# Six big loads get a wait on a later VectorE instruction: attention and a token-mixing MLP on one Trainium2 core

## The chip, the cores and the metric

The kernel runs on one core of one Trainium2 chip. The core has five engines with a queue of instructions each: TensorE (PE in the profile, with its weight loads as PEld), VectorE (DVE), ScalarE (ACT), GpSimd (POOL) and SyncE (SP). SP and POOL are used here mainly to issue DMA transfers, and all transfers run on the core's 16 DMA engines. The metric is the device time of one execution in microseconds. The kernel before was run three times: 746.62, 742.23 and 740.57 us, median 742.23.

## The reference

One input x of 2048 rows and 640 columns is normalised by row. It goes through a self-attention with 32 heads of 20 columns and, beside it, through an MLP that mixes rows (tokens) rather than columns. The result is x plus the attention's output times silu of the MLP's output.

```python
def _A_ref(x, wqkv, wo):                     # 32 heads, Dh = 20
    qkv = (x @ wqkv).reshape(B, S, 3, H, Dh)  # S = 2048
    q, k, v = ...
    p = softmax(einsum("bhqd,bhkd->bhqk", q, k) * Dh ** -0.5)
    o = einsum("bhqk,bhkd->bhqd", p, v)
    return o.reshape(B, S, D) @ wo
def _B_ref(x, w1, b1, w2, b2):
    h = layernorm(x)
    u = gelu(einsum("bsd,sf->bdf", h, w1) + b1)   # w1: 2048 x 1536
    return (einsum("bdf,fs->bds", u, w2) + b2).transpose(0, 2, 1)   # w2: 1536 x 2048
xn = layernorm(A_x)
return A_x + _A_ref(xn, ...) * silu(_B_ref(xn, ...))
```

## The kernel before

**The planner.** The program is not written in the order in which it runs. `_Kern.schedule` builds jobs (scores, exponentials, products with v, the MLP, the output projection) and picks the next instruction of each engine with a clock of its own. Each instruction or transfer is a `_Task` with an engine, a start `t0` and an end `fin` on that clock, and the tasks that it has to wait for (`waits`, one per counter). `klg` holds, for each counter, how far a task is known to be done once this one is done. At the end `emit` writes each engine's tasks in order: first one semaphore wait for each entry of `waits`, then the instruction. Only tasks with `need_inc` raise their semaphore. What runs on the chip is a fixed order for each engine and a fixed set of waits; the planner's clock only chose them.

**The attention.** The heads are taken in 8 groups of four, and the queries in four blocks of 512. For each key chunk of 128 the scores of a head go to a PSUM bank (line 1362). Three quarters of the exponentials are ACT's (line 1392, into pt_sb). The others are made on DVE as bit patterns: line 1403 turns scores into a 16-bit pattern in dt_sb, and then three shifted copies of that tile are needed. A copy is made either on DVE (line 1471, adding a constant) or by an accumulating DMA that adds a constant tile from HBM to the tile in place (`emit_x`, line 1434, task names dX...). That accumulating transfer is issued by POOL; it moves 512 KB. It works in place, so it starts only when PE has read the tile's earlier state, and PE waits for its landing before it reads the tile again. The products with v (line 1497) read pt_sb and dt_sb, and accumulate four copies of a tile with scaled v (v_sb, vs_sb).

**The MLP.** It runs as bank jobs between the attention's instructions: m1_0 to m1_11 with w1, a gelu on ACT, then m2_0 to m2_15 with w2 (lines 715 and 723; results picked up at lines 887 and 896, then lines 920 to 925). The weights come in pieces of two column chunks: w1_0 to w1_5 (1024 KB each, line 850) and w2_0 to w2_7 (768 KB each, line 857), in two slots of regA. Piece k is loaded when the chunks that used piece k - 2 are done, so w1_2 goes out behind m1_1 and is read by m1_4 and m1_5.

**SP's queue.** SP issues all other transfers in the planner's order, and a task that waits holds up all behind it. Of interest are the weight pieces, the load of wo (line 1794) and the four small pieces of line 1797 right behind it, the last x rows for the residual (x2_3, line 1789, into regA), the four stores of each pass's attention output (line 1639), the stores and loads of q and k through HBM (lines 745, 770 and 784), and late in the program 16 transposing loads (line 1006). Transfers use eight counters in turn, so a transfer also waits for the one eight places ahead.

Of the kernel before, what the change touches and what calls it, by code (L numbers as in the profile page):

```python
# [283 lines left out]
class _Kern:  # L284
# [8 lines left out]
    AB = 6  # L293
    JB = 7
    EVJ = 36.0
    XRES = 12
    RC = (1, 4, 7, 10, 13)
    NT = 2
# [66 lines left out]
        ("JOBF", (4, 0, 8)),  # L365
        ("EVJ", (36.0, 19.0, 45.0)),
        ("XLEFT", (16, 20, 14, 28, 99)),
# [33 lines left out]
    def __init__(self, nc, A_x, A_wqkv, A_wo, B_w1, B_b1, B_w2, B_b2, out):  # L401
# [10 lines left out]
        self.FC = self.F // 128  # L412
        self.prog = Prog(nc)

    def build(self):
        nc = self.nc
        pr = self.prog
        S, NB, FC = self.S, self.NB, self.FC
        es = ExitStack()
        with es:  # L420
            E = es.enter_context
            bf, f32, u16 = dt.bfloat16, dt.float32, dt.uint16
            t = {}

            def sb(name, shape, d):
                t[name] = E(nc.sbuf_tensor(name, shape, d))

            sb("wqk_sb", [P, 5, 2, 640], bf)
            sb("wp_sb", [P, 5, 2, 128], bf)
            sb("qs_sb", [P, self.NQS, 512], bf)  # L430
            sb("wv_sb", [P, 5, 640], bf)
            sb("xnT_sb", [P, 5, S], bf)
            sb("regA", [P, NB, self.D], bf)
            sb("regB", [P, FC, self.D], bf)
            sb("regC", [P, NB, self.D], bf)
            sb("qk_sb", [P, 2, 2, S], bf)
            sb("v_sb", [P, NB, self.H, 22], bf)
            sb("vs_sb", [P, 2, 3, len(self.RC), 88], bf)
            sb("pt_sb", [P, self.RP, 512], bf)
            sb("dt_sb", [P, self.NTILE, 4, 512], u16)  # L440
            sb("kc_sb", [P, 2, 64], u16)
            sb("zt_sb", [P, 2, 2, self.D], bf)
            sb("tr_sb", [P, 512], f32)
            sb("on_sb", [P, 16, 32], bf)
            sb("rden_sb", [P, 16], f32)
            sb("stage_sb", [P, 3, 512], bf)
            sb("idb_sb", [P, P], bf)
            sb("zw_sb", [P, 32], bf)
            sb("bst_sb", [P, NB, 12], f32)
            sb("st_sb", [P, 8, NB], f32)  # L450
            sb("cst_sb", [P, 4], f32)
            sb("b1h_sb", [P, FC], f32)
            sb("b2h_sb", [P, NB], f32)
            sb("bload_sb", [P, FC + NB], bf)
            t["ps_all"] = E(nc.psum_tensor("ps_all", [P, 4096], f32))
            t["qk_dram"] = nc.dram_tensor("qk_scratch_dram", [2, 560, S], bf)
            t["oT_dram"] = nc.dram_tensor("oT_scratch_dram", [8 * P, S], bf)
            t["kc_dram"] = nc.dram_tensor("kc_scratch_dram", [2 * P, 2048], dt.uint8)
            t["ok_dram"] = nc.dram_tensor("ok_scratch_dram", [S, 512], bf)
            sems = {}  # L460
            for e in ("pe", "act", "dve", "pool", "sp"):
                sems[e] = E(nc.semaphore(f"sem_{e}"))
            for i in range(pr.n_lanes):
                sems[f"d{i}"] = E(nc.semaphore(f"sem_d{i}"))
            for i in range(pr.NXL):
                sems[f"x{i}"] = E(nc.semaphore(f"sem_x{i}"))
            self.t = t
            self.schedule()
            pr.final_waits()
            pr.emit(sems)  # L470
# [6 lines left out]
    def schedule(self):  # L477
        pr, t, nc = self.prog, self.t, self.nc
# [594 lines left out]
        def res_steps(b):  # L1073
            def make(bk):
                r = regC[:, b, :]
                xa = regA[:, b, :]
                if b < self.XRES:
                    return [("xdma", lambda e: e.dma_start(r, A_x[0, b * 128:(b + 1) * 128, :], accum_op=ALU.add),
# [649 lines left out]
        for b in range(NB):  # L1728
            at = self.V1A + (self.V1B - self.V1A) * b / NB
            rest.append((at, f"v1_{b}", v_steps(b, 1), xtag(b // 4), 40.0, at))  # L1730
        for i, (a0, a1) in enumerate(self.QC):
            o = [(1, tb) for tb in range(4)] + [(0, tb) for tb in range(4)]
            for n, (w, tb) in enumerate(o if i < 4 else o[:4]):
                at = a0 + (a1 - a0) * n / (8.0 if i < 4 else 4.0)
# [4 lines left out]
        for G in range(1, NG):  # L1739
            cs = sorted({(80 * G - 80) // 128, (80 * G - 1) // 128})  # L1740
            for w in (1, 0):
# [5 lines left out]
                    at=(4 * G - 1.0 if G < NG - 1 else 24.0))  # L1747
# [35 lines left out]
        for gb in range(4):  # L1783
            if 4 * gb + 4 <= self.XRES:
                x2.append(("tag", f"x2_{gb}"))
# [407 lines left out]
        def do_step(j, eng):  # L2193
            s = j.steps[j.i]
            j.i += 1
            if s[0] == "ev":
                n = s[8]
                fn = ev_fn(s, eng)
                cost = ac(n) if eng == "act" else (dv(n, 0.53) if s[7].startswith("xTe") else dp(n))
                getattr(pr, eng)(fn, reads=s[5], writes=s[6], name=s[7], cost=cost)  # L2200
                if eng == "dve":
                    done_cost["dve"] += cost
            elif s[0] == "pe":
                done_cost["pe"] += s[5]
                if len(s) > 6:
                    c = pe_cost("pv", s[5])
                    for fn in s[1]:
                        pr.pe(fn, reads=s[2], writes=s[3], name=s[4], cost=c / len(s[1]), w=s[5] / len(s[1]))
                else:
                    pr.pe(s[1], reads=s[2], writes=s[3], name=s[4], cost=pe_cost("full", s[5]), w=s[5])  # L2210
            else:
                getattr(pr, s[0])(s[1], reads=s[2], writes=s[3], name=s[4], cost=s[5])
                if s[0] in done_cost:
                    done_cost[s[0]] += s[5]
            settle(j)

        def eng_cands(eng, T):
            c = []
            for j in active:
                s = j.steps[j.i]  # L2220
                if s[0] == eng:
                    p_ = min(j.prio, self.EVJ) if eng == "dve" and j.bk is not None and not ramp[0] else j.prio
                    c.append((p_, pr.ready(eng, s[2], s[3]), lambda j=j: do_step(j, eng)))
# [41 lines left out]
        while True:  # L2265
# [41 lines left out]
            r, e = bt  # L2307
# [5 lines left out]
        assert nclaim[0] == NALL and not avail and not dquads and not jobs and not bankq and not active, (  # L2313
            nclaim[0], len(avail), len(dquads), [j.name for j in jobs][:9], [j.name for j in bankq][:9],
            [j.name for j in active][:9], pv_pass, pv_left)
        self.model = dict(pr.T)
        self.stats = stats

# [35 lines left out]
```

## Time and profile before

| | us |
|---|---|
| three runs, median | 742.23 |
| lowest and highest run | 740.57, 746.62 |
| the profiled execution's own time | 746.19 |
| its span in the profile | 744.4 |
| mean granted TensorE clock, as a share of full | 0.995 |

The rows shown below are of one profiled execution. A row of a timeline gives start and length in us, the engine, the line of the kernel, the operation, the tile written and the tile read, how many instructions are merged in the row, and in brackets how long the engine was idle before it and what ended that. SPq and the POOL rows of line 1434 are issues of transfers; how long a transfer takes from issue to landing is told in a row of its own. A row of a table by stretch gives the stretch, its length, and the busy time of PE, PEld, DVE, ACT and POOL with the number of instructions, then the granted TensorE clock, the busy share of the DMA engines and the GB/s. A busy PE is not PE at its peak, since matmuls are pipelined.

### The profile page before, as it was taken

Reading aid. Unit: us, or ns where it says so; the run is one execution under the profiler, and the core shown is the slowest. Engines: PE = TensorE matmul, PEld = TensorE weight load, DVE = VectorE, ACT = ScalarE, POOL = GpSimd, SP = SyncE. Lnnn points to the kernel's source line nnn. Section 1 sums busy time; section 2 is a strip of 40 time slices with the busy share of each in tenths; the row PEclk is TensorE's granted clock in tenths of the full one; section 3 lists DMA queues with packets and bytes.
Section 4 is the critical chain, followed back from the end, with each engine's and each line's share of the span. In section 5 each row is a group of like instructions: output and inputs, shape, how many; then the busy total and the mean of one; then the engine's idle time right before and its main releaser. Section 6 shows DMA issues by size and latency. Waiting matters only on the chain.

```text
span 744.4 us, 23686 instructions
## 1 busy us (share of the span) xinstructions
PE 709.4 (95%) x10506; PEld 236.9 (32%) x10520; DVE 701.0 (94%) x1286; ACT 715.5 (96%) x711; POOL 91.5 (12%) x107
## 2 busy tenths in 40 slices
PE   8889999999989999999899999899999999999997
PEld 7332222222322232322322323233333333332233
DVE  7989999999978999989889999899999999999997
ACT  5999999999989999999999999999999999999995
POOL 4300000100002001001101001110110101102311
PEclk9999999999999999999999999999999999999999
DMA  8767544542456554455463446824668785445443
GB/s 238 147 129 106 122 77 92 85 83 48 86 118 113 84 118 80 92 118 105 77 140 50 90 65 131 181 44 121 130 128 132 129 157 116 82 105 98 92 90 92
DMA packets 134091, 79.90 MB, mean 107 GB/s; under 512 B 84564, under 2 KB 123860, under 8 KB 133940
## 3 DMA queue, kind: packets, MB, share of 16 engines
q0 software_dynamic: 11808, 38.67, 28.6%
q1 hardware_dynamic: 122180, 39.71, 25.3%
q8 instruction: 82, 1.34, 0.8%
q14 instruction: 21, 0.17, 0.1%
HBM read 44.72 MB, written 10.75 MB: 75 GB/s over the span
## 4 chain that ended last, share of the span: by engine, by line
ACT 69%; PE 17%; DMA 6%; DVE 6%; issue 1%; SPq 0%; DVEq 0%
ACT pt_sb L1392 67%; PE ps_all L1497 5%; PE ps_all L1362 5%; DMA dt_sb<-kc_scratch_dram 4%; PE ps_all L715 4%; DVE dt_sb L1403 2%; PE ps_all L1036 1%; ACT zt_sb L920 1%; ACT regB L907 1%; DMA regA<-in_A_x_dram 1%; DVE dt_sb L1471 1%; DMA xnT_sb<-oT_scratch_dram 1%; DMA xnT_sb<-regC 1%; DMA oT_scratch_dram<-stage_sb 1%; DVE bst_sb L596 0%
## 5 line engine op out<-in xcount | busy, mean ns | idle before, releaser
L1392 ACT ACTIVATE pt_sb<-ps_all 128x1024 bf16<-128x1024 f32 (+1 forms) x682 | 692.1, 1210 | 12.0 <-PE ps_all L1362 9.4
L1403 DVE TENSOR_SCALAR dt_sb<-ps_all 128x512 uint16<-128x512 f32 x540 | 357.3, 680 | 24.6 <-PE ps_all L1362 16.3
L1362 PE MATMUL ps_all<-qk_sb 32*128 32x512 bf16 (+1 forms) x2128 | 269.5, 377 | 15.1 <-ACT pt_sb L1392 13.7
L1471 DVE TENSOR_SCALAR dt_sb<-dt_sb 128x2048 uint16<-128x2048 uint16 x335 | 222.3, 685 | 3.9 <-PE ps_all L1497 2.8
L1362 PEld LDWEIGHTS ps_all<-qk_sb 32*128 32x128 bf16 x2128 | 68.0, 91 | 274.2 <-ACT pt_sb L1392 222.7
L1497 PE MATMUL ps_all<-dt_sb,vs_sb 128*21 128x512 bf16 (+1 forms) x1668 | 144.0, 379 | 4.8 <-DMA dt_sb<-kc_scratch_dram 4.5
L1434 POOL DMA_DIRECT2D dt_sb<-kc_scratch_dram x70 | 64.9, 928 | 576.6 <-PE ps_all L1497 248.4
L1497 PE MATMUL ps_all<-pt_sb,v_sb 128*21 128x512 bf16 (+1 forms) x1572 | 120.6, 375 | 1.4 <-DVE v_sb L1190 0.8
L715 PE MATMUL ps_all<-regC,regA 128*32 128x128 bf16 (+1 forms) x1432 | 69.9, 296 | 1.5 <-issue 1.5
L715 PE MATMUL ps_all<-regB,regA 128*32 128x512 bf16 (+1 forms) x1464 | 65.7, 297 | 1.1 <-DVE qs_sb L765 0.6
L1497 PEld LDWEIGHTS ps_all<-dt_sb,vs_sb 128*21 128x21 bf16 x1668 | 36.1, 90 | 63.3 <-issue 39.7
L1497 PE MATMUL ps_all<-dt_sb,v_sb 128*21 128x512 bf16 (+1 forms) x556 | 53.3, 378 | 0.1
L715 PE MATMUL ps_all<-xnT_sb,wqk_sb 128*32 128x512 bf16 x640 | 48.9, 383 | 0.2 <-DVE v_sb L1190 0.2
L1497 PEld LDWEIGHTS ps_all<-pt_sb,v_sb 128*21 128x21 bf16 x1572 | 28.4, 91 | 42.7 <-issue 33.2
L723 PE MATMUL ps_all<-regC,regA 32*128 32x512 bf16 x104 | 40.4, 388 | 0.0
L715 PEld LDWEIGHTS ps_all<-regC,regA 128*32 128x32 bf16 x1432 | 27.6, 96 | 23.8 <-issue 14.6
L715 PEld LDWEIGHTS ps_all<-regB,regA 128*32 128x32 bf16 x1464 | 27.1, 96 | 25.1 <-issue 12.9
L723 PE MATMUL ps_all<-regB,regA 32*128 32x512 bf16 x72 | 27.7, 384 | 0.0
L1036 PE MATMUL ps_all<-wv_sb,xnT_sb 128*128 128x128 bf16 (+1 forms) x148 | 25.0, 294 | 2.4 <-issue 0.9
L1625 DVE STREAM_TRANSPOSE tr_sb<-ps_all 128x512 f32<-128x512 f32 x31 | 21.9, 707 | 0.1
L715 PE MATMUL ps_all<-wv_sb,xnT_sb 128*32 128x480 bf16 x320 | 21.8, 369 | 0.0
L1497 PEld LDWEIGHTS ps_all<-dt_sb,v_sb 128*21 128x21 bf16 x556 | 13.7, 90 | 20.2 <-issue 16.0
(88 smaller groups left out, 339.9 us busy)
## 6 DMA issues: line engine op xcount, KB each, us to landing
dt_sb<-kc_scratch_dram POOLq DMA_DIRECT2D x70, 512.0 KB, 6.3
regA<-in_B_w_dram SPq DMA_DIRECT2D x6, 1024.0 KB
regA<-in_B_w_dram SPq DMA_DIRECT2D x8, 768.0 KB
qk_sb<-qk_scratch_dram SPq DMA_DIRECT2D x56, 80.0 KB
qk_scratch_dram<-qs_sb SPq DMA_DIRECT2D x32, 128.0 KB
regA<-in_A_x_dram SPq DMA_DIRECT2D x3, 640.0 KB
ok_scratch_dram<-on_sb SPq DMA_DIRECT2D x96, 20.0 KB
regC<-in_A_x_dram POOLq DMA_DIRECT2D x12, 160.0 KB, 4.4
```

Source lines behind the costliest of these rows:

```text
L715: fns.append(lambda e, c=c, e_=e_: e.matmul(oc(c, e_), lhsT[:, c:e_], rhs, start=start, stop=stop, tile_position=(0, c)))
L723: row = lambda g: (lambda e: e.matmul(oc(0, 128), lhsT[32 * g:32 * g + 32, :], rhs[32 * g:32 * g + 32, :], start=False, stop=False, tile_p ...
L907: steps.append(("act", lambda e, d=d: e.activation(d, d, AF.Gelu_apprx_tanh), [S_(f"u{f}_{q}") for f in range(f0, f0 + 3) for q in (0, 1)] ...
L920: steps.append(("act", lambda e: e.activation(tt_, z, AF.Tanh), sz, [stt], f"th2_{j}", ac(n)))
L1036: steps.append(("pe", lambda e, c=c: e.matmul(ap, oT_sb[:, c, b * 128:(b + 1) * 128], wo_ap[:, c, c0:c0 + n], start=(opens and c == 0), st ...
L1362: t = pr.pe(lambda e, outp=outp, lhsT=lhsT, rhs=rhs, g=g: e.matmul(outp, lhsT, rhs, start=True, stop=True, tile_position=(32 * g, 0)), rea ...
L1392: tk = pr.act(lambda e: e.activation(outp, inp, AF.Exp, scale=math.log(2.0) / 128.0), reads=[bank_slot[b] for b in banks[:n]], writes=[S_( ...
L1403: tk = pr.dve(lambda e: e.tensor_scalar(w, src, WOFF, 0.0, ALU.add, ALU.max), reads=[bank_slot[bk]], writes=[S_(f"dt{d['tl'][0]}_{g}")], n ...
L1434: t = pr.xdma(lambda e: e.dma_start(dst, src, accum_op=ALU.add), [S_(f"kc{i}")] + sl_, sl_, f"dX{d['q']}_{d['c']}_{k1}")
L1471: tk = pr.dve(lambda e: e.tensor_scalar(dst, src, dk, None, ALU.add), reads=[S_(f"dt{b}_{g}") for b in inb for g in range(4)], writes=[S_( ...
L1497: pr.pe(lambda e: e.matmul(outp, lhsT, rhs, start=(k == 0), stop=last, tile_position=(0, 32 * g)), reads=reads, writes=[bank_slot[AB]], na ...
L1625: steps.append(("dve", lambda e: e.transpose(tr_sb[:, :], ps(AB)), [bank_slot[AB]], [S_("tr")], f"epT{q}", 632.0))
```

## The change

When the whole plan stands, a new function goes through SP's tasks. For each of the weight pieces, wo and the x2 loads it looks on the planner's clock whether the load is due from 3.0 us before to 5.0 us after the issue of an accumulating transfer. If so, it moves the due time to 5.0 us after that transfer, and on to the next one if it meets that too. The due time is cut off 8.5 us ahead of the first task that waits for the load, and 0.6 us ahead of the next SP task (not counting the small wo pieces). Then it takes the last DVE instruction that starts behind the load's old due time and ends by the new one, and that depends on nothing SP issues from here on, and makes the load wait for it. Six loads get such a wait. The order on every engine, and all other waits, stay.

```diff
+    XBEF, XAFT, LNEED = 3000.0, 5000.0, 8500.0
...
+    def calm_loads(self):
+        pr = self.prog
+        sp = [t for t in pr.tasks["sp"] if t.fn is not None]
+        xs = [t.t0 for t in pr.tasks["pool"] if t.name.startswith("dX")]
+        users = {}
+        for e in pr.tasks:
+            for t in pr.tasks[e]:
+                for w in t.waits.values():
+                    users.setdefault(id(w), []).append(t.t0)
+        for i, t in enumerate(sp):
+            if not t.name.startswith(("dma_w1_", "dma_w2_", "x2_")) and t.name != "wo":
+                continue
+            at = t.t0
+            for x in sorted(xs):
+                if x - self.XBEF < at < x + self.XAFT:
+                    at = x + self.XAFT
+            if at == t.t0:
+                continue
+            lim = min(users.get(id(t), [1e12])) - self.LNEED
+            nxt = next((u for u in sp[i + 1:] if not u.name.startswith("wo7")), None)
+            if nxt is not None:
+                lim = min(lim, nxt.t0 - 600.0)
+            at = min(at, lim)
+            late = [u for u in sp[i:]]
+            best = None
+            for d in pr.tasks["dve"]:
+                if d.fn is None or d.t0 < t.t0:
+                    continue
+                if d.fin > at or any(d.klg[pr.cidx_of[u.ceng]] >= u.cidx for u in late):
+                    break
+                best = d
+            if best is not None:
+                t.waits["dve"] = best
+                best.need_inc = True
+                self.moved.append((t.name, t.t0, best.fin))
...
+        self.calm_loads()
         self.model = dict(pr.T)
```

More of the change, by code (lines that the diff above doesn't have):

```diff
@@ L413, in __init__ @@
         self.prog = Prog(nc)
+    def calm_loads(self):
[33 more added lines that the diff above has]
+                self.moved.append((t.name, t.t0, best.fin))
     def build(self):
         nc = self.nc
+        self.moved = []
         pr = self.prog
```

## The prediction

> **What bounds the kernel now.** I read the page's chain shares first, then the chain in order of time, then the timelines around its DMA pieces, last the landing time of single transfers. The page:
>
> ```profile
> PE 709.4 (95%) x10506; PEld 236.9 (32%) x10520; DVE 701.0 (94%) x1286; ACT 715.5 (96%) x711; POOL 91.5 (12%) x107
> ACT 69%; PE 17%; DMA 6%; DVE 6%; issue 1%; SPq 0%; DVEq 0%
> dt_sb<-kc_scratch_dram POOLq DMA_DIRECT2D x70, 512.0 KB, 6.3
> ```
>
> Three engines are over 93% busy and ACT carries 69% of the chain, so little can be won: mainly the pieces where all three stand still. In the chain those are the long waits for an accumulating transfer (dt_sb from kc_scratch, line 1434, issued by POOL, read by PE at line 1497). The last row gives 70 of them with a median landing of 6.3 us. Three stand in the chain (start, length):
>
> ```profile
> 205.58 10.81 DMA dt_sb<-kc_scratch_dram
> 319.16 9.27 DMA dt_sb<-kc_scratch_dram
> 596.00 9.18 DMA dt_sb<-kc_scratch_dram
> ```
>
> What the first two cost, in the timelines of PE and ACT (in brackets the idle time before the row), and TensorE's granted clock in the stretch behind the first:
>
> ```profile
> 216.44 0.40 PE L1497 MATMUL ps_all<-dt_sb,vs_sb 128*21 128x512 bf16 x4 [2.65 <-DMA dt_sb<-kc_scratch_dram]
> 328.48 0.40 PE L1497 MATMUL ps_all<-dt_sb,vs_sb 128*21 128x512 bf16 x4 [1.14 <-DMA dt_sb<-kc_scratch_dram]
> 217.19 2.10 ACT L1392 ACTIVATE pt_sb<-ps_all 128x1024 bf16<-128x1024 f32 x2 [2.63 <-PE ps_all L1362]
> 219.78 1.02 ACT L1392 ACTIVATE pt_sb<-ps_all 128x1024 bf16<-128x1024 f32 x1 [0.48 <-PE ps_all L1362]
> 221.28 107.07 ACT L1392 ACTIVATE pt_sb<-ps_all 128x1024 bf16<-128x1024 f32 x107 [0.47 <-PE ps_all L723]
> 329.23 39.87 ACT L1392 ACTIVATE pt_sb<-ps_all 128x1024 bf16<-128x1024 f32 x40 [0.89 <-PE ps_all L1362]
> 217.00:221.50 4.50, 4.50 (x46) 0.92 (x47) 2.86 (x5) 3.29 (x4) 0.00 (x0) 0.62 0.18 38
> ```
>
> The reader is to see a stall of 2.65 us on PE, ACT empty for the same time, and then PE at a clock of 0.62 for 4.5 us, so that ACT starves twice more.
>
> **The change part by part.** Nothing is removed or reordered. Six SP loads get one more wait each, on a DVE instruction, and that instruction signals. Which six follows from the diff's rule on the planner's own due times (written on the tasks of the kernel before; they choose the instruction, no time below is taken from them): w1_2, w1_4, wo, w2_3, w2_4 and x2_3 (the last a load of x rather than of weights). w1_3, w1_5, w2_0, w2_1, w2_2 and w2_7 stand outside the rule's stretch around any transfer; w2_5 and w2_6 have a transpose due behind them at once, so no later DVE instruction fits. Hence the third chain piece, at 596.00, stays as it is: the load ahead of it is w2_6. The issues now, with what is queued behind two of them, and the DVE instructions waited for:
>
> ```profile
> 205.42 0.44 SPq L850 DMA_DIRECT2D regA<-in_B_w_dram  x1
> 228.08 1.92 SPq L1639 DMA_DIRECT2D ok_scratch_dram<-on_sb  x4
> 317.47 0.95 SPq L850 DMA_DIRECT2D regA<-in_B_w_dram  x1
> 498.67 0.44 SPq L1794 DMA_DIRECT2D wv_sb<-in_A_wo_dram  x1
> 499.25 2.67 SPq L1797 DMA_DIRECT2D wqk_sb<-in_A_wo_dram  x4
> 502.02 0.39 SPq L857 DMA_DIRECT2D regA<-in_B_w_dram  x1
> 523.01 0.40 SPq L857 DMA_DIRECT2D regA<-in_B_w_dram  x1
> 544.16 0.40 SPq L857 DMA_DIRECT2D regA<-in_B_w_dram  x1
> 211.69 1.29 DVE L1471 TENSOR_SCALAR dt_sb<-dt_sb 128x2048 uint16<-128x2048 uint16 x2
> 322.38 1.42 DVE L1471 TENSOR_SCALAR dt_sb<-dt_sb 128x2048 uint16<-128x2048 uint16 x2
> 502.01 0.34 DVE L896 TENSOR_SCALAR zt_sb<-ps_all,b2h_sb 128x128 bf16<-128x128 f32 x1
> 532.40 0.95 DVE L833 TENSOR_SCALAR vs_sb<-v_sb 128x440 bf16<-128x440 bf16 x3
> 548.06 0.48 DVE L923 TENSOR_SCALAR zt_sb<-zt_sb 128x1280 bf16<-128x1280 bf16 x1
> ```
>
> Single transfers near them, each issue row followed by its own landing time:
>
> ```profile
> 207.95 0.87 POOL L1434 DMA_DIRECT2D dt_sb<-kc_scratch_dram  x1 [1.50 <-PE ps_all L1362]
> DMA to landing us min/median/max: 11.2/11.2/11.2
> 228.31 0.87 POOL L1434 DMA_DIRECT2D dt_sb<-kc_scratch_dram  x1 [19.48 <-PE ps_all L1497]
> DMA to landing us min/median/max: 7.2/7.2/7.2
> 315.49 0.88 POOL L1434 DMA_DIRECT2D dt_sb<-kc_scratch_dram  x1 [14.91 <-PE ps_all L715]
> DMA to landing us min/median/max: 6.3/6.3/6.3
> 362.21 0.87 POOL L1434 DMA_DIRECT2D dt_sb<-kc_scratch_dram  x1 [0.39 <-PE ps_all L1362]
> DMA to landing us min/median/max: 9.7/9.7/9.7
> 547.04 1.18 POOL L1434 DMA_DIRECT2D dt_sb<-kc_scratch_dram  x1 [2.70 <-DVE dt_sb L1471]
> DMA to landing us min/median/max: 7.7/7.7/7.7
> ```
>
> w1_2. The load goes out at 205.42, 0.16 us ahead of the transfer at 205.58 (landing 10.8) and 2.5 us ahead of the one at 207.95 (11.2). It will wait for the first of the two DVE instructions at 211.69, so until about 212.4, 7.0 us later. The nearest row without a load beside it is the transfer at 228.31, which also starts right behind four stores (228.08): 7.2. So the first transfer should land near 212.8, and PE wants it at 216.44 - 2.65 = 213.79. The stall goes as long as it lands within 8.2 us. The gain is read on PE, which is what the chain follows there: 2.65 idle, and 4.5 x (1 - 0.62) = 1.71 of clock that the stall took away, 4.36 in all. Read on ACT it is 2.63 + 0.48 + 0.47 = 3.58. I take 4.36, because ACT's gaps behind the stall come from the slow PE. Bounds: 0, if the transfer lands as late as before, and 4.36. Behind the waiting load stand the stores of 228.08, far later than 212.4; w1_2 itself is first read behind m1_3, whose end also lets w1_3 go, much later. If that cover were gone, each us late would be a us of PE.
>
> w1_4. It goes out at 317.47, 1.7 us ahead of the transfer at 319.16, and will go at 322.38 + 1.42 = 323.8. The transfer at 315.49, with the load 2.0 us behind it, landed in 6.3; with that, 319.16 lands at 325.5, wanted at 328.48 - 1.14 = 327.34. The margin is 1.9 us. Gain: ACT's 0.89 (the chain behind it is ACT, and PE's clock holds). Bounds: 0 and PE's 1.14. Its own first reader, m1_8, comes only behind m1_6 and m1_7, and the next entry on SP is a store made later than the wait.
>
> wo, and what is queued behind it. From 498.67 to 502.01 + 0.34 = 502.35, 3.7 us later. The four pieces of line 1797 (2.67) and then w2_2 (502.02) move with it, w2_2 to about 505.7. Its reader:
>
> ```profile
> 525.76 0.60 PE L715 MATMUL ps_all<-regB,regA 128*32 128x512 bf16 x8
> 546.53 0.83 PE L715 MATMUL ps_all<-regB,regA 128*32 128x512 bf16 x12
> 555.22 0.40 PE L1497 MATMUL ps_all<-dt_sb,vs_sb 128*21 128x512 bf16 x4
> ```
>
> w2_2 is read at 525.76 (first row), 20 us after its new issue; even the slowest transfer above, 11.2, leaves 8.9. Cost 0; no transfer that wo slowed is waited for, so gain 0.
>
> w2_3. From 523.01 to about 532.7 (first third of the 0.95 at 532.40). It is read at 546.53: 13.8 us, against 11.2 a margin of 2.6. Cost 0; past the margin each us is one of PE.
>
> w2_4. From 544.16 to 548.06 + 0.48 = 548.5. Here the rule's limit stops it 1.5 us behind the transfer at 547.04, so it still goes beside it. That transfer lands at 554.74 and is read at 555.22: only 0.5 us of slack, the thinnest place. The nearest row is 315.49: a load 2.0 us behind a transfer left it at 6.3. I take 0; the lower bound is the second rival. The load's own reader is m2_8, two chunks behind the one at 546.53.
>
> x2_3. It moves by a few us and is read only at the very end, by the last residual additions. Cost 0.
>
> The waits themselves. Six signals on DVE and six conditions on SP, which has nothing else to do at these points. No row shows a signal as time of its own; if each cost a tenth of the 0.34 us instruction at 502.01, six were 0.2 us. I take 0.
>
> Sum: 4.36 + 0.89 = 5.25 us. The profiled execution took 746.19 (span 744.4); without these it would take 740.9. The median of the three runs is 742.23, 3.96 below the profiled one, and both stalls follow from the order of issue, so I take them to be in every run: 742.23 - 5.25 = 737.0.
>
> **The rivals.** First, the load isn't what makes the transfer late (the change doesn't do what it says). For it: the transfer at 362.21 took 9.7 with no weight load beside it, only stores and another transfer just ahead; the transfers at 205.58 and 207.95 also have four stores ahead. Against it: 228.31, with such stores, landed in 7.2, and 315.49 in 6.3 while 319.16, a load in between, took 9.3. Then both stalls stay and the time is 742.2. [...]
>
> Second, the w2_4 load stretches the transfer at 547.04 (the other side). If a load that comes 1.5 us behind hurts it as much as one ahead, it lands as late after the load as 207.95 did in total: 548.5 + 11.2 = 559.7, 4.5 us after 555.22. With the clock price of the first stall (1.71 per 2.65, so 1.65 us per us idle) that is 7.4; less the gain of 5.25 it ends at 744.4. It decides from 5.25 / 1.65 = 3.2 us of stall, so a landing after 558.4. Against it stands the 6.3 at 315.49. [...]
>
> **How the numbers follow.** The forecast (both stalls gone, nothing new) gets 0.71, at 737.0; its gain lies between 3.58 (the first stall read on ACT, the second hidden) and 5.50 (the second read on PE), so its own span is 736.7 to 738.7. No effect, 742.2: 0.17. The w2_4 stall, 742 to 744.4: 0.07. The remaining 0.05 is for something that isn't in these rows. The runs of before lie 1.7 below to 4.4 above their median, so the range reaches from 733 (the largest gain, 736.7, less 1.7 of scatter and 2 for a median of few runs) to 743.5 (no effect, and some scatter), which leaves out the upper end of the second rival. A measurement of this kernel can tell about 1%, 7.4 us, from no change: faster than 734.8 is more than the rows give and needs scatter on top, 0.14; slower than 749.7 needs more than any one rival, 0.03; within, 0.83.
>
> **What would show it.** In the changed profile: the two chain pieces at 205.58 and 319.16 gone, no idle PE before line 1497 there, PE's clock at 1.00 in the stretch behind; those transfers at 6 to 8 us; SP's loads about 7.0 and 6.3 us later against them; the piece near 596 unchanged; no PE idle before the rows of 525.76, 546.53 and 555.22. Wrong it would be if the landings stay over 9 us although the load is gone, if a new wait for dt_sb appears near 555, or if both stalls go and ACT's busy share doesn't rise, because PE or DVE then set the pace.

## The result and the profile after

| | before | after |
|---|---|---|
| median of seven runs, us | 743.22 | 738.15 |
| lowest and highest run, us | 740.57, 746.62 | 737.39, 740.31 |
| the profiled execution, us | 746.19 | 738.15 |
| its span, us | 744.4 | 736.4 |

The ratio of the runs is 0.9928, with a 95% interval of 0.9903 to 0.9953: 5.07 us less by the medians, which is inside the 1% that counts as the same. The two profiled executions differ by 8.04 us. The ratios here and below are of undisturbed executions; one of e4's, the one that was profiled, ran at a granted clock of 0.75 and took 828.05 us, and nothing is read from it. Line numbers of the kernel after are higher by 38 (line 1434 is line 1472, 1392 is 1430, 1497 is 1535), and by 39 in e6, e7, e8 and e10 to e12.

The page after, with the lines that answer to those shown of before:

```profile
PE 705.8 (96%) x10506; PEld 236.2 (32%) x10520; DVE 700.7 (95%) x1286; ACT 714.9 (97%) x711; POOL 91.5 (12%) x107
ACT 76%; PE 14%; DMA 4%; DVE 4%; SPq 1%; issue 0%; DVEq 0%
dt_sb<-kc_scratch_dram POOLq DMA_DIRECT2D x70, 512.0 KB, 6.0
```

Busy times hardly moved (ACT 715.5 to 714.9), the shares did: the chain is 76% ACT instead of 69%, and the DMA's share fell from 6 to 4%.

SP's timeline after, with the loads w1_2 and w1_4:

```profile
212.19 0.41 SPq L888 DMA_DIRECT2D regA<-in_B_w_dram  x1
...
319.37 0.41 SPq L888 DMA_DIRECT2D regA<-in_B_w_dram  x1
```

The two transfers that these loads stood ahead of, in the view of line 1472 (length of the issue in ns, and its start), each with its landing time:

```profile
L1472 POOL DMA_DIRECT2D dt_sb<-kc_scratch_dram x1: 872/872/872, 205.3 to 205.3; - x1
DMA to landing us min/median/max: 6.0/6.0/6.0
...
L1472 POOL DMA_DIRECT2D dt_sb<-kc_scratch_dram x1: 1027/1027/1027, 314.7 to 314.7; - x1
DMA to landing us min/median/max: 6.0/6.0/6.0
```

They landed after 10.8 and 9.3 us before, and after 6.0 now. In ACT's timeline after there is one row for both places, with no idle time inside it to speak of, and in the table by stretch PE's clock is whole:

```profile
37.55 420.32 ACT L1430 ACTIVATE pt_sb<-ps_all 128x1536 bf16<-128x1536 f32 x419 [0.48 <-PE ps_all L1535]
```

```profile
217.00:221.50 4.50, 4.22 (x60) 0.96 (x52) 4.47 (x8) 4.50 (x7) 0.00 (x0) 1.00 0.04 9
```

The only piece of the chain after that still waits for such a transfer is the third one, behind w2_6, which did not move:

```profile
587.88 9.28 DMA dt_sb<-kc_scratch_dram
```

**How the stages are compared.** The kernel's instructions run in the same order in every version, so the time from one POOL transfer to a later one measures the stage between them. The rows of before and of after that give the stage of w1_4 (the same is done below with the transfers at 205.58 and 228.31, and with those of other stages):

```profile
319.16 1.02 POOL L1434 DMA_DIRECT2D dt_sb<-kc_scratch_dram  x1 [2.80 <-DVE dt_sb L1471]
336.71 1.03 POOL L1434 DMA_DIRECT2D dt_sb<-kc_scratch_dram  x1 [16.53 <-DVE dt_sb L1471]
```

```profile
314.65 1.03 POOL L1472 DMA_DIRECT2D dt_sb<-kc_scratch_dram  x1 [2.80 <-DVE dt_sb L1509]
330.94 1.03 POOL L1472 DMA_DIRECT2D dt_sb<-kc_scratch_dram  x1 [15.26 <-DVE dt_sb L1509]
```

That is 17.55 us before and 16.29 after: 1.26 won. All profiled executions, in us (a stage is named by its two transfers in the profile of before; "end" is from the last transfer, at 703.25, to the end of the span):

| kernel | 205.58-228.31 (w1_2) | 319.16-336.71 (w1_4) | 362.21-383.08 | 497.72-521.86 (wo) | 596.00-612.07 (w2_6) | end | span |
|---|---|---|---|---|---|---|---|
| before | 22.73 | 17.55 | 20.87 | 24.14 | 16.07 | 41.15 | 744.4 |
| before again (e5) | 22.65 | 19.48 | 18.70 | 24.54 | 16.73 | 41.02 | 744.2 |
| after | 18.49 | 16.29 | 17.89 | 24.94 | 16.17 | 41.18 | 736.4 |
| after again (e9) | 18.49 | 16.29 | 18.54 | 24.93 | 16.52 | 46.62 | 742.5 |
| w1_2 alone (e1) | 18.50 | 19.36 | 18.78 | 24.14 | 16.19 | 41.27 | 740.0 |
| w1_4 alone (e2) | 22.47 | 16.28 | 18.48 | 24.14 | 15.38 | 40.98 | 738.9 |
| the other four (e3) | 22.12 | 16.95 | 18.38 | 24.14 | 16.30 | 41.20 | 740.9 |
| w1_2 between (e6) | 18.50 | 17.62 | 18.14 | 24.14 | 16.29 | 40.99 | 737.9 |
| w1_2 just behind (e7) | 18.50 | 17.94 | 18.79 | 24.14 | 15.39 | 44.95 | 740.5 |
| six and w2_6 (e8) | 18.49 | 16.28 | 18.12 | 24.73 | 15.39 | 40.98 | 737.1 |
| six and w2_6 (e11) | 18.50 | 16.28 | 18.38 | 24.14 | 15.38 | 41.46 | 735.3 |
| five and w2_6 (e10) | 18.49 | 16.28 | 18.36 | 24.61 | 15.39 | 40.96 | 737.9 |
| columns behind (e12) | 18.49 | 16.28 | 17.84 | 24.74 | 16.65 | 45.08 | 740.4 |

Between the first two profiles, 4.24 us come from the stage of w1_2 and 1.26 from that of w1_4. Another 2.98 come from the third stage, where the change does nothing, and 0.80 are lost in the stage of wo. The stages of w1_2, w1_4, wo and w2_6 repeat to 0.01 us in the profiles in which nothing stalls in them; the others are read against that floor (18.49, 16.28, 24.14, 15.38).

### The profile page after: what moved, and what is told of

Its sections match the earlier page's. It is cut to its first block, busy times and chain, and to the rows that moved or that the text cites. A ratio compares the mean times of both kernels' runs of the same rounds, so it can differ in the third digit from the quotient of the medians.

```text
span 736.4 us, 23688 instructions
## 1 busy us (share of the span) xinstructions
PE 705.8 (96%) x10506; PEld 236.2 (32%) x10520; DVE 700.7 (95%) x1286; ACT 714.9 (97%) x711; POOL 91.5 (12%) x107
## 3 DMA queue, kind: packets, MB, share of 16 engines
q0 software_dynamic: 11808, 38.67, 28.5%
## 4 chain that ended last, share of the span: by engine, by line
ACT 76%; PE 14%; DMA 4%; DVE 4%; SPq 1%; issue 0%; DVEq 0%
ACT pt_sb L1430 74%; PE ps_all L1535 5%; PE ps_all L1400 4%; PE ps_all L753 3%; DVE dt_sb L1441 2%; DMA dt_sb<-kc_scratch_dram 1%; DMA regA<-in_A_x_dram 1%; PE ps_all L1074 1%; ACT zt_sb L958 1%; ACT regB L945 1%; DMA xnT_sb<-oT_scratch_dram 1%; DVE dt_sb L1509 1%; DMA oT_scratch_dram<-stage_sb 1%; DMA xnT_sb<-regC 0%; SPq L579 0%
```

## The experiments

Medians of all runs, each against the kernel before on the same chip:

| kernel | median, us | before there, us | ratio, 95% interval |
|---|---|---|---|
| e1: w1_2 alone | 740.55 | 744.58 | 0.9953 (0.9935 to 0.9970) |
| e2: w1_4 alone | 741.54 | 744.58 | 0.9965 (0.9933 to 0.9996) |
| e3: wo, w2_3, w2_4, x2_3 | 743.77 | 744.58 | 0.9989 (0.9967 to 1.0011) |
| e4: all but wo | 738.97 | 744.58 | 0.9945 (0.9921 to 0.9968) |
| e6: w1_2 between | 741.76 | 744.67 | 0.9959 (0.9930 to 0.9988) |
| e7: w1_2 just behind | 740.78 | 744.67 | 0.9952 (0.9931 to 0.9974) |
| e8: six and w2_6 | 737.75 | 744.67 | 0.9903 (0.9875 to 0.9930) |
| e9: the change again | 739.86 | 745.45 | 0.9932 (0.9906 to 0.9957) |
| e11: as e8 | 738.20 | 745.45 | 0.9925 (0.9892 to 0.9957) |
| e10: five and w2_6 | 738.47 | 745.45 | 0.9913 (0.9883 to 0.9943) |
| e12: columns behind | 742.64 | 744.92 | 0.9977 (0.9949 to 1.0005) |

The kernel before itself was profiled once more (e5, 745.98 us).

### Which loads matter: e1 to e4

Only the list of loads that may wait differs; e2 names w1_4, e3 names wo, w2_3, w2_4 and x2_3, e4 all but wo:

```diff
-            if not t.name.startswith(("dma_w1_", "dma_w2_", "x2_")) and t.name != "wo":
+            if t.name not in ('dma_w1_2',):
                 continue
```

> Only w1_2 waits, all else as before. Theory (a load issued ahead of an accumulating transfer makes it late): the two transfers near 205 and 208 land in 6 to 7.5 us, PE has no idle before reading dt_sb near 216, its clock stays at 1.00, and the time is 4.2 us below the kernel before (3.6 to 4.8); the stall of 1.1 us near 328 stays. Rival (the gain is mostly PE's pauses for its own instructions, which come and go between runs): the time is less than 2 us below.

> Only w1_4 waits. Theory: the transfer near 319 lands in about 6 us and not 9.3, the 10.8 us one near 205 stays, and the time is about 1.2 us below the kernel before (0.5 to 1.8). Rival (instruction pauses): no difference, or as large as with w1_2 alone.

> Only wo, w2_3, w2_4 and x2_3 wait. Theory: nobody waited for the transfers that these loads slowed, so nothing is gained, and the wo and w2_2 loads, moved beside a fetch of PE's instructions near 506, cost about 0.7 us there: time from 0 to 0.8 us above the kernel before. Rival (every load beside a transfer costs time): 1 to 3 us below.

> All waits of the change but the one on wo. Theory: as with the whole change, but without PE's pause of 0.7 us behind the wo load: 5.5 to 6.2 us below the kernel before, so 0.5 to 0.8 better than the whole change. Rival (that pause is chance and not the load's doing): the same as the whole change, 5.1 below, with the pause there or somewhere else.

Each wait takes away its own stall and leaves the other (table of stages): e1 has 18.50 and 19.36, e2 has 22.47 and 16.28. The last four take away neither, though their loads did delay transfers: the one that w2_3 stood ahead of (523.97 in the kernel before) landed after 9.0 us there and after 6.2 in e3, the one at 547.04 after 7.7 and 5.5, the one at 659.09 after 7.6 and 5.1 (x2_3 goes out 0.17 us behind that one in the kernel before). Nobody waited for these.

The medians are coarser. e1 is 4.03 us below the kernel before, as expected. e2 is 3.04 below, above its expected 0.5 to 1.8; its interval reaches from 0.3 to 5.0 us, so the medians alone do not tell w1_4 from w1_2, and the stages do. e3 is 0.81 below where 0 to 0.8 above was expected, and its ratio cannot be told from 1; the cost of 0.7 us near wo did not show (stage 24.14). e4 is 5.61 below, which fits both its theory (5.5 to 6.2) and its rival (5.1).

### What it is about the load: e6 and e7

w1_2 alone waits, on an earlier DVE instruction than in the change. In e6 the load goes out between the two transfers near 205 and 208 us, in e7 (with 206600.0) just behind the second:

```diff
+            at = {'dma_w1_2': 204800.0}.get(t.name, at)
```

> Only w1_2 gets a wait, on a VectorE instruction planned to end near 204.7, so that it should be issued near 206.9: about 1.3 us behind the accumulating transfer of 205.6 and about 1 us ahead of the one of 207.95. Theory (it is the order that counts: a transfer issued behind a load waits for the load's queued packets, one issued ahead of it does not): the first transfer lands after 6 to 7 us as with the full wait, the second after 9 to 11 us; what reads the second comes some 4 us later than what reads the first, so that little of its delay is waited for; the lead over the kernel before rises by 3 to 4.2 us at this place. Rival (the two share the 16 engines packet by packet, whichever came first): the first lands after 8.5 us or more, TensorE stands for over 1 us, and the lead rises by 2.5 us at most.

> Only w1_2 gets a wait, on a VectorE instruction planned to end near 206.6, so that it should be issued near 208.8: less than 1 us behind the second of the two accumulating transfers, 3.2 us behind the first and 3.5 us earlier than in the change. Theory of the order: both transfers land after 6 to 7.5 us, no wait for them at this place, and the lead rises by 4.2 us, as with the load at 212. Rival (sharing packet by packet): the second lands after 8.5 us or more and the first after 7 or more; the lead rises by 2 to 4 us.

e6: SP's timeline, and then the two transfers in the view of their line, with landing times:

```profile
206.81 0.41 SPq L889 DMA_DIRECT2D regA<-in_B_w_dram  x1
```

```profile
L1473 POOL DMA_DIRECT2D dt_sb<-kc_scratch_dram x1: 872/872/872, 205.4 to 205.4; - x1
DMA to landing us min/median/max: 6.5/6.5/6.5
...
L1473 POOL DMA_DIRECT2D dt_sb<-kc_scratch_dram x1: 872/872/872, 207.8 to 207.8; - x1
DMA to landing us min/median/max: 9.5/9.5/9.5
```

e7, the same:

```profile
208.04 0.41 SPq L889 DMA_DIRECT2D regA<-in_B_w_dram  x1
```

```profile
L1473 POOL DMA_DIRECT2D dt_sb<-kc_scratch_dram x1: 872/872/872, 204.8 to 204.8; - x1
DMA to landing us min/median/max: 6.1/6.1/6.1
...
L1473 POOL DMA_DIRECT2D dt_sb<-kc_scratch_dram x1: 875/875/875, 207.2 to 207.2; - x1
DMA to landing us min/median/max: 7.2/7.2/7.2
```

In e6 the load of 1024 KB delayed the transfer that was issued 1.0 us behind it (9.5) and hardly the one issued 1.4 us ahead of it (6.5; 5.8 to 6.1 in the profiles with no load near). In e7, with the load 0.8 us behind, the second transfer takes 7.2, inside the 6.8 to 7.4 of the profiles with the load 4.5 us behind. So 0.8 us of distance behind the transfers would have done here, where the change waits for 4.5. Both kernels keep the 18.50 of the first stage, e6 because its late second transfer is read only later. By the medians they lead by 2.9 and 3.9 us.

The packets in the DMA view show how the order acts. Queue q0 (software_dynamic) carries POOL's transfers, q1 (hardware_dynamic) SP's: q0's 38.67 MB on the pages before and after are those of POOL's 70 transfers of 512 KB and 12 loads of 160 KB. From 208.5 to 210.5 us only one of them moves: in the kernel before SP's, though the transfer has been issued at 205.58, and in e6, where the load was issued 1.4 us behind it, POOL's (packets, MB, share of the 16 engines' time):

```profile
q1 hardware_dynamic: 525, 0.27, 74.1%
```

```profile
q0 software_dynamic: 87, 0.36, 92.8%
```

Later, from 213 to 217 us, both move in the kernel before:

```profile
q0 software_dynamic: 198, 0.75, 92.6%
q1 hardware_dynamic: 198, 0.10, 12.2%
```

So what had been issued second stood still at first in both, and in the kernel before it moved beside the other later. The first packet of the transfer at 205.58 moved 6.2 us after its issue in the kernel before, and 1.9 us after it in the kernel after (issue at 205.31). Why it stood still at first is not shown.

In that stretch of the kernel before the two queues moved 198 packets each, q0's of 4 KB but for 16 small ones, q1's of 0.5 KB. The earlier stretch, in which one queue moved alone, is what made the order count here: the 4.3 us by which the transfer's first packet came later in the kernel before are most of the 4.8 by which it landed later (10.8 and 6.0).

How far behind was enough differed by place. A load of 768 KB (w2_3) 0.6 to 1.2 us behind the transfer at 521.86 left it at 6.6 to 7.8 us, against 5.9 to 6.1 with no load near, and x2_3, 0.17 us behind its transfer, at 7.4 to 7.8 against 4.9 to 5.3. In e1, where the 7.8 was measured, the load's packets moved first although its issue came 0.6 us later.

### Is the pause at 368 us part of it: e5

The third stage holds no wait that the change touched. In the chain of the first profile of before it is this piece, time in which PE waited for nothing that the profile shows:

```profile
368.36 1.54 issue
```

> The kernel before, unchanged, for a second profile. Theory: the transfers issued at 205.6 and 319.2 land after 9 us or more again and stop the chain, by some 4 and 1 us; the pause of TensorE near 368 us, where no transfer, no load and no wait is near, comes again with another length (ScalarE idle between 0 and 3 us there), since it is chance. Rival: the pause has the 2.8 us of the first profile again, and then it belongs to the kernel before and the change took it away.

The pause came again and was smaller. ACT's timeline of e5 there:

```profile
371.30 9.21 ACT L1392 ACTIVATE pt_sb<-ps_all 128x1024 bf16<-128x1024 f32 x9 [0.91 <-PE ps_all L1362]
```

The stage took 18.70 instead of 20.87, and in the other kernels 17.84 to 18.79. So the 2.98 us that the first two profiles differ by here are not the change's. Part of the 20.87 is the clock, which fell behind the pause in the first profile of before only:

```profile
371.28:374.69 3.41, 3.41 (x34) 0.79 (x31) 2.06 (x6) 2.62 (x3) 0.00 (x0) 0.50 0.22 75
```

No run changes the pause, but the packets of the traces tell more of it. The profile's DMA queues hold one of instructions:

```profile
q8 instruction: 82, 1.34, 0.8%
```

Its 82 packets of 16 KB are 64 bytes for each of the 21,026 instructions of PE and PEld, so it is taken for the loading of PE's instructions. PE comes to the place of the pause 6.1 to 6.2 us behind the transfer at 362.21. Where the packet ahead of that place had ended by 5.0 us (the DMA view of a narrow window gives its time), the pause was 0.27 us at most (after, e8, e12); at 5.1 to 5.6 us it was 0.39 to 0.70, at 5.8 to 5.9 it was 0.95 to 1.03 (e1, e5, e7), and at 6.2 it was 1.54 (before). In the stage of wo, PE comes to the place of its pause 8.2 us behind the transfer at 497.72. In the seven profiles in which the packet had ended by 5.4 to 6.1 us there is no pause, in the six in which it ended at 7.2 to 7.5 there is one of 0.34 to 0.72. So both pauses go with a packet of this queue that ends late. Why the packet is late in one execution and not in another is not shown.

e5 also shows how much one execution says of a stall. The stage of w1_4 took 19.48, 1.93 more than in the first profile of before. PE's idle time there, and its clock in two stretches, the one with the idle time and the one behind it:

```profile
328.27 0.40 PE L1497 MATMUL ps_all<-dt_sb,vs_sb 128*21 128x512 bf16 x4 [1.58 <-DMA dt_sb<-kc_scratch_dram]
```

```profile
325.38:328.79 3.41, 1.83 (x26) 0.51 (x22) 2.41 (x4) 2.32 (x3) 0.00 (x0) 1.00 0.27 53
328.79:332.20 3.41, 3.41 (x29) 0.61 (x26) 2.08 (x3) 2.05 (x2) 0.00 (x0) 0.50 0.00 0
```

1.58 us of idle PE halved the clock here; 1.14 did not in the first profile. The same rows of e1:

```profile
324.70 0.40 PE L1535 MATMUL ps_all<-dt_sb,vs_sb 128*21 128x512 bf16 x4 [1.46 <-DMA dt_sb<-kc_scratch_dram]
```

```profile
321.88:325.29 3.41, 1.95 (x26) 0.51 (x22) 2.46 (x4) 2.37 (x3) 0.00 (x0) 1.00 0.19 39
325.29:328.70 3.41, 3.41 (x29) 0.61 (x26) 2.08 (x3) 2.05 (x2) 0.00 (x0) 0.50 0.00 0
```

and of e7:

```profile
323.88 0.40 PE L1536 MATMUL ps_all<-dt_sb,vs_sb 128*21 128x512 bf16 x4 [1.52 <-DMA dt_sb<-kc_scratch_dram]
```

```profile
319.70:323.11 3.41, 2.66 (x39) 0.72 (x31) 2.92 (x5) 3.41 (x4) 0.00 (x0) 1.00 0.63 125
323.11:326.52 3.41, 2.64 (x37) 0.77 (x41) 1.98 (x4) 2.14 (x3) 0.00 (x0) 1.00 0.00 0
```

Nearly the same idle time; e1's clock fell and its stall cost 19.36 - 16.28 = 3.08 us, e7's held and cost 1.66. The stretches are cut where the traces let the clock change: in the thirteen profiles of the table above it is 1.00 or 0.50, and it changes only at whole multiples of 3.41 us from its first rise. In e5 and e1 the idle time lies in one such step, and PE is busy for 1.83 and 1.95 us of it. In e7 a border at 323.11 cuts the idle time in two, and PE is busy for 2.66 and 2.64 us of the two steps. Over all thirteen profiles, from 30 us on, the clock fell after each step with 1.95 us of busy PE or less, and after none with 2.02 or more; in the first 30 us three steps with 1.70 to 1.81 kept it. So the place of a stall against the steps decided here, which looks like chance in a single profile. A fall lasted one step (two in e9's profile), and in the stages of w1_2 and w1_4 the stall then cost 1.6 us more than its idle time, whether that was short or long: 3.08 for 1.46 us in e1, 3.20 for 1.58 in e5, 4.24 for 2.65 in the first profile of before.

### The third stall: e8, e11, e10

w2_6 joins the list and gets a due time by hand. e11 is the same kernel once more, beside the whole change (e9) on one chip; e10 leaves wo out:

```diff
+            if t.name not in ('dma_w1_2', 'dma_w1_4', 'wo', 'dma_w2_3', 'dma_w2_4', 'x2_3', 'dma_w2_6'):
                 continue
...
+            at = {'dma_w2_6': 584300.0}.get(t.name, at)
```

> The whole change, and w2_6 waits as well, on a VectorE instruction that ends near 589.5, 1.7 us behind the accumulating transfer of 587.9. Theory: that transfer lands after 6 to 7 us instead of 9.3, the wait of 0.8 us of the chain of waits there goes, and the time is 0.8 us below that of the whole change (some 5.9 us below the kernel before); the transposes queued behind w2_6 on SyncE slip by some 5 us and are not waited for. Rival: w2_6 or those transposes become late, and a new wait of 1 us or more shows within 15 us behind that place; the time is the whole change's or above.

> The whole change, unchanged, for a direct comparison on one chip and for a second profile. Theory: in the profile no wait at the two transfers near 205 and 315, the third one near 588 lands after 9 us and is waited for by 0.8 us; the median is 5 to 6 us below the kernel before, and the pauses of TensorE near 368 and 498 us come or not with other lengths than in the first profile of it (0 and 0.7 us). Rival: the pause near 498 has 0.7 us again and the one near 368 is 0 again, so that both belong to the order of the change.

> The whole change and a wait for w2_6 too, the same kernel as the run that gave 737.75 us, now beside the whole change on one chip. Theory: the transfer near 588 lands after 6 to 7 us, its wait of 0.8 us is gone, and the median is 0.4 to 1.0 us below that of the whole change, at the edge of what the runs can tell. Rival: the two medians agree within 0.3 us, or this one is above.

> The change without the wait for wo, and with a wait for w2_6. Theory: wo's wait is worth nothing either way (the transfer of 497.7 landed after 8.4 to 8.8 us with and without it, and nobody waited for it), so the time is that of the six waits with w2_6, within 0.5 us. Rival: wo's wait is part of a pause of TensorE near 498 us, and without it the time is 0.5 to 0.8 us lower.

In e8's timeline of SP the load now stands behind the transfer, which lands after 6.6 us instead of 9.3:

```profile
591.38 0.38 SPq L896 DMA_DIRECT2D regA<-in_B_w_dram  x1
```

```profile
L1473 POOL DMA_DIRECT2D dt_sb<-kc_scratch_dram x1: 872/872/872, 589.7 to 589.7; - x1
DMA to landing us min/median/max: 6.6/6.6/6.6
```

Its stage is 15.38 to 15.39 in all three kernels, against 16.17 and 16.52 in the two profiles of the change: 0.8 to 1.1 us, and no new wait behind it. In the medians that is not settled. e8 is 0.4 us below the first median of the change, e11 1.7 (0.4 to 1.0 was expected) and e10 1.4 below that of e9 on the same chip, with ratios whose intervals overlap. So these versions do not show as slower than the change, and by the profile they are better in one stage. e10, without wo's wait, is within 0.3 us of e11, as its theory said. Of the two pauses, e9 shows the one in the stage of wo with the same length as the first profile of the change (24.93 and 24.94), and the one at 368 us with another (18.54 and 17.89).

One thing here stays open. In e2 and e7 w2_6 was issued 2.61 and 2.65 us ahead of that transfer and did not delay it (7.0 and 7.1); in e1 and e6, 2.84 and 2.86 us ahead, it did (9.3 and 9.4). So 0.2 us more of lead went with 2.3 us more until the landing, which the order alone does not explain. The load's bytes are the same. w1_4 at 2.65 us ahead did delay its transfer (8.7, in e3).

### A race at the end: e9's profile and e12

The second profile of the change took 742.5 us, 6.1 above the first; 5.44 of it lie behind the last transfer ("end", 46.62). The chain there in the first profile of the change, and in e9:

```profile
695.69 5.20 DMA xnT_sb<-oT_scratch_dram
```

```profile
696.69 7.71 DMA xnT_sb<-oT_scratch_dram
```

It is a load of 80 KB, issued by SP and read by the output projection. POOL issues two accumulating residual loads (x rows into regC) at the same moment. In the first profile they go out 0.28 us behind SP's load, in e9 0.06 us ahead of it:

```profile
695.97 2.42 POOL L1116 DMA_DIRECT2D regC<-in_A_x_dram  x2
```

```profile
696.63 2.42 POOL L1116 DMA_DIRECT2D regC<-in_A_x_dram  x2
```

The price in e9 is idle time on PE and then half the clock, in the timeline and the table by stretch:

```profile
704.45 0.61 PE L1074 MATMUL ps_all<-wv_sb,xnT_sb 128*128 128x512 bf16 x1 [3.45 <-DMA xnT_sb<-oT_scratch_dram]
```

```profile
703.82:710.65 6.83, 5.87 (x42) 1.27 (x44) 3.12 (x5) 3.57 (x4) 0.00 (x0) 0.50 0.29 99
```

To see whether the order does it, e12 forces the bad one: the whole change, and SP's load waits on one more DVE instruction.

```diff
-            if not t.name.startswith(("dma_w1_", "dma_w2_", "x2_")) and t.name != "wo":
+            if not t.name.startswith(("dma_w1_", "dma_w2_", "x2_")) and t.name not in ("wo", "oTl72_4_48"):
...
+            at = 689100.0 if t.name == "oTl72_4_48" else at
...
-                if d.fn is None or d.t0 < t.t0:
+                if d.fn is None or d.fin < t.t0:
```

> The whole change, and one more wait, at the end: the load of 80 KB from oT_scratch into xnT_sb (issued at 695.69 in the changed kernel, 0.28 us ahead of POOL's two accumulating residual loads at 695.97, landing after 5.2 us) waits on a VectorE instruction that ends near 696.45, so that it comes 0.5 us behind the first of the two. In two of eleven profiles it came 0.06 and 0.11 us behind by chance and landed after 7.7 and 7.2 us. Theory of the order: it lands after 7.2 us or more, TensorE stands for 3 us or more and ScalarE after it, the granted clock falls to about half for some 5 us, and the whole run is 4.5 to 6.5 us above the changed kernel's (743 to 745 us). Rival (those two were late by something else): it lands after 5.0 to 5.5 us, and the run is longer by the 0.8 us of the later issue alone, 1 us at most.

POOL's loads went out at 696.07. e12's chain of waits, PE's timeline and its clock behind it:

```profile
696.65 6.84 DMA xnT_sb<-oT_scratch_dram
```

```profile
703.54 0.60 PE L1075 MATMUL ps_all<-wv_sb,xnT_sb 128*128 128x512 bf16 x1 [3.10 <-DMA xnT_sb<-oT_scratch_dram]
```

```profile
703.57:706.98 3.41, 3.41 (x25) 0.57 (x25) 1.40 (x3) 1.78 (x2) 0.00 (x0) 0.50 0.57 197
```

The direction is the theory's, the sizes are below it: landing 6.84 instead of 7.2 or more, and 45.08 - 41.18 = 3.9 us instead of 4.5 to 6.5. The clock fell for one step of 3.41 us, where it fell for 6.83 us in e9. By the issue itself SP's load is 0.86 us later against the last transfer (696.65 - 695.32, where it was 695.69 - 695.22); a rival of 1 us at most does not give 3.9. The median, 742.64, is 4.49 above the change's first and 2.78 above its second. Over the profiles, SP's load landed after 4.88 to 5.24 us when it was issued ahead of POOL's or up to 0.05 us behind (before: 0.05; e1: 0.03), and after 7.71, 7.19 and 6.84 at 0.06, 0.11 and 0.58 us behind (e9, e7, e12). So a few hundredths of a us decide over 3.8 to 5.4 us here (44.95 and 46.62 against 41.18), and the change sets neither of the two issues. A wait that forces the good order was not tried.

## Why the prediction was right, and where it was off

It gave 737.0 us, a range of 733 to 743.5, and the same within 1% as the likeliest. It was 738.15.

- **w1_2, 4.36 taken: 4.24.** Right in mechanism and size. Reading the stall on PE, idle time and lost clock, gave the answer; ACT's 3.58 would have been too small. In the profiles in which it stayed, the stall cost between 3.63 (e3) and 4.24.
- **w1_4, 0.89 taken: 1.26 in the same profile, and 0.67 to 3.20 in the others (e3 and e5, against 16.28).** This term was mis-sized. The step that failed is "the chain behind it is ACT, and PE's clock holds": the clock held in that execution, where the price was PE's idle time of 1.14 and 0.12 more, and it fell in e5 and e1. A stall of about 1.5 us made it fall in e1 and e5 and not in e7, by its place against the steps of 3.41 us, so its price is a spread, which one profile cannot give. The upper bound of 1.14 was too low even for its own profile.
- **The third stall, left as it is: right** (9.2 before, 9.3 after).
- **w2_3, w2_4 and x2_3, cost and gain 0: right.** The thin place, w2_4 1.5 us behind the transfer at 547.04, landed after 5.2 us instead of 7.7.
- **wo, 0: right as far as the runs show.** Its stage was 24.73 to 24.94 in four of the six profiles with wo's wait, and 24.14 in the other two; without the wait it was 24.14 in five, and 24.54 and 24.61 in two (e5 and e10). What goes with the longer stage is the late packet of instructions, with the wait and without it. It cost the profiled execution 0.8 us, which the sum had no term for. Whether the wait makes the packet late more often stays open.
- **The base.** The sum was taken from a median of three runs, 742.23; seven runs give 743.22. With that the forecast would have been 743.22 - 5.25 = 737.97, 0.18 from the measured time. So nearly all of the miss is the base. That the rest is so small is partly luck: the interval of the gain reaches from 3.5 to 7.2 us, and w1_4's price alone varies by 2.5. The two profiles, 8.0 us apart, would have misled: 2.98 of that is the pause at 368 us.
- **The first rival** (the load does not make the transfer late) fell in e1, e2, e6 and e7. What spoke for it, the transfer at 362.21 that took 9.7 with no load beside it, fits the order too: another accumulating transfer goes out 1.4 us ahead of it, at 360.79. That one was not tried by itself.
- **The second rival** (a load 1.5 us behind stretches the transfer) fell at the place it was made for, with 5.2, and again in e6, with 6.5. The 742 us at which its stretch begins no run shows: in the kernel after, with the load 1.58 us behind, that transfer landed after 5.2 us where it had taken 7.7. And its 1.65 us for each us of idle PE is no rate: a fall of the clock added 1.6 us to an idle time of 1.46 (e1) and of 2.65 us (before).

## What to carry to other kernels

In this kernel what counted was what had been queued ahead. Before a transfer on which the chain waits, look for the large loads issued ahead of it (in the kernel before 0.16, 1.69 and 3.72 us ahead of transfers that landed after 10.8, 9.3 and 9.2 us), and let them go behind it, 1 to 2 us rather than far away (in the kernel after 1.30 and 1.58 us behind transfers that landed after 6.0 and 5.2 us), and then read its landing again. A stall of TensorE cost its idle time here, and 1.6 us more where the clock fell behind it (4.24 for 2.65 us, 3.08 for 1.46); size such a term from several executions. Where two queues issue within 0.1 us of each other and one of the two transfers is waited for, look at their order in several profiles, because here it changed from one execution to the next (SP's load 0.28 us ahead in the first profile of the change, 0.06 us behind in e9); in e12 a wait set it.

## What the runs showed of the hardware

- In the thirteen profiles a transfer of 512 KB that adds in place landed after 8.8 to 10.8 us where a load of 768 or 1024 KB had been issued 0.15 to 1.7 us ahead of it, and after 5.1 to 8.1 when that load came 0.6 to 2 us behind. The exception is w2_7: 1.0 to 1.5 us ahead of the transfer at 615.75 it left it at 6.8 to 7.4, against 5.3 to 5.8 in the eight profiles in which it came later. A transfer issued 1.4 to 1.5 us behind another of its kind was late without a weight load ahead: 8.3 to 9.7 at 362.21 and 8.3 to 8.8 at 497.72, over all thirteen profiles.
- From 213 to 217 us in the kernel before, packets of both queues were moving, 198 of each, which gave the queue with 4 KB packets 92.6% of the engines' time and the one with 0.5 KB packets 12.2%.
- The clock fell to 0.50, in steps of 3.41 us, behind 1.46 us of idle PE in e1 and 1.58 in e5, and not behind 1.52 in e7, which two steps shared. It fell already after a step with less than half of it idle (1.95 of 3.41 us busy in e1).
- PE paused at the same two places in most of the thirteen profiles and with another length each time (at 368 us the stage took from 17.84 to 20.87). The pause was the longer the later a 16 KB packet of the instruction queue ended (0.27 us or less up to 5.0 us behind the transfer at 362.21, 1.54 us at 6.2). No run changed this.
